# Holding the sums of a fused attention kernel to the plan, moving the first of them to GpSimd, and spreading the half products

## The chip, the cores and the metric

The kernel runs on one core of a Trainium2 chip. The metric is the device time of one execution in microseconds (us), given as the median of several executions. The profile is one execution, recorded instruction by instruction. Engine names are those of the profile: PE is TensorE, PEld its weight loads, DVE is VectorE, ACT is ScalarE, POOL is GpSimd, SP is SyncE. The profile lists a stream of instructions for each engine (8145 on PE and 1788 on DVE in the kernel before) and the semaphore events that ended its waits. What a wait means for DVE is seen in the profile below: while it stood 6.03 us before one instruction, nothing behind that instruction ran on it. The *granted clock* is the share of PE's full clock that the profile records as granted (0.959 in the mean in the kernel before).

## The reference, cut to what matters

```python
# u, v: 8 x 3008 x 256;  z: 8 x 3008 x 64;  w_in: 256 x 2048;  w_out: 2048 x 256
scores = (1/3008) * z @ z.T                 # per batch, symmetric
attn   = maximum(scores, 0) ** 2
x      = u * (attn @ v)                     # 24064 rows of 256
h      = x @ w_in
out    = (h * cos(h)) @ w_out
```

Because `scores` is symmetric, only the tiles with row block R at or after column block c are computed. The others are made by a DMA that transposes a finished tile (the first three columns of the first batch are an exception: all their tiles are computed).

## The kernel before

Each batch has six columns of 512 tokens, numbered from 0 (the last has 448). A column is planned as 8 units of time, and every piece of work is given a place in that plan. The pieces are emitted in the order of the plan; a scheduler then decides the order on each engine. The matmuls are chained, so PE keeps the planned order. The other engines are not chained.

```python
def chain(mm):                       # fixes the order of the PE stream
    if before:
        after(mm.ins, before.pop(), NOSYNC)
    before.append(mm.ins)
```

For columns 2 to 5 (3 to 5 in the first batch) the part of `attn @ v` that uses transposed tiles is made with seven half products instead of eight, for up to four row blocks W ("four-row columns" below are columns 4 and 5). That needs sums of quarters of the tiles. The *first sums* are two per tile, and the first of them writes in place:

```python
def a_sums1(b, c, R):                # 102 tiles, so 204 first sums
    s1 = quarter(b, c, R, 0, 1)
    nc.vector.tensor_tensor(s1, s1, quarter(b, c, R, 1, 1), ALU.add)
    nc.vector.tensor_tensor(
        second(b, c, R), s1, quarter(b, c, R, 0, 0), ALU.subtract)

def a_sums2(b, c, R):                # the second sums, later in the column
    # ...
    nc.vector.tensor_tensor(dst, src, sub, ALU.subtract)
# ... in the plan of a column that begins at unit t:
at(t - 2.5 + 0.5 * i, 2, lambda b=b, c=c, R=R: a_sums1(b, c, R))
at(t + 1.5 + 0.3 * i, 2, lambda b=b, c=c, R=R: a_sums2(b, c, R))
for n, o in ((1, 1.0), (5, 1.0), (2, 1.0), (6, 1.4), (7, 3.0), (3, 3.0), (4, 3.4)):
    at(t + o, 2, lambda b=b, c=c, n=n: product(b, c, n))
    # ... keep(): ACT and DVE take partial products out of PSUM
```

Three more kinds of DVE work matter. The *squares* are `s <- rt * rt`, 128x1024, with both inputs in SBUF. The products *g* are `h * cos(h)`, with one input in PSUM. The *finish x* is `acc * u`, also with one input in PSUM. Six PSUM buffers `w` serve the scores, h and the output; a score visit takes all six. Two buffers `acc` serve the column. GpSimd issues the loads and makes sums of v (`v_sums`).

## Time and profile before

The time before is 1403.17 us (median of 3, 1401.99 to 1404.43). The profiled execution is a further one, of 1409.64 us with a span of 1407.9 us.

| | busy us | share of the span |
|---|---|---|
| PE | 1272.8 | 90% |
| DVE | 955.0 | 68% |
| ACT | 885.3 | 63% |
| POOL | 234.6 | 17% |

PE is the bound. These are the groups of PE instructions of the kernel before that show idle time. The columns are busy time and mean ns of one, then the idle time of PE just before them and what ended it.

```profile
L324 PE MATMUL acc<-s,v 128*128 128x512 f16 (+1 forms) x1392 | 345.2, 386 | 10.4 <-DVE x L347 10.4
L419 PE MATMUL acc<-s,vsum 128*128 128x256 f16 (+1 forms) x816 | 112.5, 279 | 19.5 <-ACT q L439 9.4 <-ACT p L432 8.2 <-DVE s L391 1.0
L236 PE MATMUL w<-zT 64*128 64x512 f16 (+3 forms) x684 | 109.9, 374 | 63.3 <-DVE g L458 46.8 <-DVE rt L267 12.8 <-ACT zT L199 1.6
L419 PE MATMUL acc<-s,v 128*128 128x256 f16 (+1 forms) x612 | 87.2, 286 | 37.5 <-DVE x L347 37.5
```

With 1.2 us before the first matmuls this adds up to 131.9 us of idle PE. About 108 us of it is released by DVE, although DVE is only 68% busy; most of the rest is released by ACT. So DVE is not short of time; it is late at certain moments. PE's timeline of the kernel before at one batch boundary shows two such moments (start, duration, instructions, idle time before):

```profile
660.82 0.60 PE L468 MATMUL w<-w_out,g 128*128 128x256 f16 x4
664.93 1.68 PE L419 MATMUL acc<-s,v 128*128 128x224 f16 x8 [3.51 <-DVE x L347]
...
667.77 0.93 PE L419 MATMUL acc<-s,v 128*128 128x224 f16 x8
...
687.28 0.44 PE L236 MATMUL w<-zT 64*128 64x512 f16 x3
694.44 1.18 PE L236 MATMUL w<-zT 64*128 64x256 f16 x3 [6.72 <-DVE g L458]
```

After the wait eight matmuls of one shape take 1.68 us, where eight of that shape take 0.93 us a little later: the clock was halved (the trace's clock record reads 0.5 from 664.22 to 667.63 us). The DVE timeline of the same stretch tells what DVE was doing:

```profile
655.28 2.48 DVE L458 TENSOR_TENSOR g<-w,c 128x512 f16<-128x512 f32 x4
663.79 0.42 DVE L376 TENSOR_TENSOR s<-s 128x512 f16<-128x512 f16 x1 [6.03 <-DMA s<-s]
664.13 1.41 DVE L347 TENSOR_TENSOR x<-acc,ut 128x192 f16<-128x192 f32 x4
...
685.22 1.28 DVE L458 TENSOR_TENSOR g<-w,c 128x512 f16<-128x512 f32 x2
693.17 0.62 DVE L376 TENSOR_TENSOR s<-s 128x512 f16<-128x512 f16 x1 [6.67 <-DMA s<-s]
693.72 1.27 DVE L458 TENSOR_TENSOR g<-w,c 128x512 f16<-128x512 f32 x2
```

DVE stands at a first sum (L376) whose transposing DMA has not landed, and the finish x or the products g behind it are late by as much. Over the whole span the list of waits has this line (engine and what it waited for: us in total, times, longest):

```profile
DVE s L376 <- DMA s<-s: 199.5, 72, 7.8
```

These sums are not due yet. In the built order the first sum of the second batch stands behind 40 products g on DVE. The scheduler had moved it ahead, since nothing forbade it.

### The profile page before, as it was taken

What the parts mean: (1) busy time and instruction counts of PE and PEld (TensorE: products, weight loads), DVE (VectorE), ACT (ScalarE), POOL (GpSimd) and SP (SyncE); (2) the same over time, 40 slices, a digit from 0 to 9 for tenths busy, and PEclk for the clock granted to TensorE, in tenths of its full rate; (3) what the DMA queues carried; (4) which work ended last, traced back from release to release, by engine and by line L of the source; (5) the groups of instructions that cost most, each with busy time, mean ns of one, the idle gap of its engine ahead of it and who ended that gap; (6) DMA issues with size and microseconds to landing.
All of it is one profiled execution on the core that took longest, in us unless ns stands there. A gap on an engine that the chain in (4) does not pass through costs nothing.

```text
span 1407.9 us, 22304 instructions
## 1 busy us (share of the span) xinstructions
PE 1272.8 (90%) x8145; PEld 752.0 (53%) x8145; DVE 955.0 (68%) x1788; ACT 885.3 (63%) x1702; POOL 234.6 (17%) x329
## 2 busy tenths in 40 slices
PE   6689799997999879998799987999879898899999
PEld 2136555564556545566455654556545565455666
DVE  6677567776667676676666865668656686566865
ACT  4367556665667656675566755666656666566656
POOL 6021310114001040111401013010130101300000
PEclk8799999998999989999999999999999999999999
DMA  9886766686657865766756667576675766756511
GB/s 123 137 113 106 108 104 108 105 121 102 101 104 103 125 104 83 115 109 110 110 90 104 123 92 111 101 96 121 91 111 102 99 116 91 111 102 93 90 39 46
DMA packets 484222, 144.98 MB, mean 103 GB/s; under 512 B 432400, under 2 KB 484112, under 8 KB 484112
## 3 DMA queue, kind: packets, MB, share of 16 engines
q1 hardware_dynamic: 356448, 88.73, 37.4%
q0 software_dynamic: 100400, 29.77, 21.6%
q10 hardware_dynamic: 27264, 25.06, 5.6%
q8 instruction: 64, 1.05, 0.3%
q14 instruction: 46, 0.38, 0.1%
HBM read 60.29 MB, written 24.64 MB: 60 GB/s over the span
## 4 chain that ended last, share of the span: by engine, by line
PE 70%; DMA 16%; DVE 6%; ACT 4%; issue 3%; ACTq 0%; DVEq 0%; SPq 0%
PE w L468 18%; PE w L451 18%; PE acc L324 18%; DMA s<-s 16%; PE acc L419 10%; PE w L236 5%; ACT rt L269 2%; DVE g L458 2%; DVE x L347 1%; DVE s L271 1%; DVE s L391 1%; DVE s L376 1%; PE acc L298 1%; ACT c L455 1%; ACT p L432 0%
## 5 line engine op out<-in xcount | busy, mean ns | idle before, releaser
L455 ACT ACTIVATE c<-w,pihalf 128x512 f16<-128x512 f32 x752 | 502.0, 704 | 300.7 <-PE w L451 209.9
L458 DVE TENSOR_TENSOR g<-w,c 128x512 f16<-128x512 f32 x752 | 491.2, 685 | 89.3 <-ACT c L455 86.1
L468 PE MATMUL w<-w_out,g 128*128 128x256 f16 x3008 | 453.1, 274 | 0.0
L451 PE MATMUL w<-x,w_in 128*128 128x512 f16 x1504 | 452.1, 384 | 0.0
L468 PEld LDWEIGHTS <-g 128*128 128x128 f16 x3008 | 296.5, 99 | 195.9 <-issue 7.0
L324 PE MATMUL acc<-s,v 128*128 128x512 f16 (+1 forms) x1392 | 345.2, 386 | 10.4 <-DVE x L347 10.4
L269 ACT ACTIVATE rt<-w 128x512 f16<-128x512 f32 x489 | 253.7, 615 | 110.8 <-PE w L236 99.4
L271 DVE TENSOR_TENSOR s<-rt 128x1024 f16<-128x1024 f16 x254 | 187.3, 743 | 113.7 <-ACT rt L269 113.5
L324 PEld LDWEIGHTS <-v 128*128 128x128 f16 x1392 | 130.2, 99 | 177.0 <-issue 64.6
L94 POOL DMA_DIRECT2D ust<-in_u_dram x112 | 81.4, 733 | 628.4 <-PE acc L324 617.3
L376 DVE TENSOR_TENSOR s<-s 128x512 f16<-128x512 f16 (+1 forms) x102 | 43.7, 429 | 199.6 <-DMA s<-s 199.5
L451 PEld LDWEIGHTS <-w_in 128*128 128x128 f16 x1504 | 149.0, 99 | 52.9 <-issue 6.7
L236 PE MATMUL w<-zT 64*128 64x512 f16 (+3 forms) x684 | 109.9, 374 | 63.3 <-DVE g L458 46.8
L419 PE MATMUL acc<-s,vsum 128*128 128x256 f16 (+1 forms) x816 | 112.5, 279 | 19.5 <-ACT q L439 9.4
L419 PE MATMUL acc<-s,v 128*128 128x256 f16 (+1 forms) x612 | 87.2, 286 | 37.5 <-DVE x L347 37.5
L419 PEld LDWEIGHTS <-vsum 128*128 128x128 f16 x816 | 79.7, 101 | 51.1 <-issue 42.9
L253 ACT ACTIVATE rt<-w 128x512 f16<-128x512 f32 (+3 forms) x176 | 63.6, 448 | 57.9 <-PE w L236 57.9
L419 PEld LDWEIGHTS <-v 128*128 128x128 f16 x612 | 62.6, 104 | 48.6 <-DVE x L347 37.3
L236 PEld LDWEIGHTS <-zT 64*128 64x128 f16 x684 | 26.0, 95 | 113.3 <-issue 100.6
L475 ACT ACTIVATE ob<-w 128x256 f32<-128x256 f32 x188 | 71.3, 379 | 5.3 <-PE w L468 5.3
L347 DVE TENSOR_TENSOR x<-acc,ut 128x64 f16<-128x64 f32 (+7 forms) x178 | 68.9, 431 | 3.6 <-PE acc L324 3.5
L391 DVE TENSOR_TENSOR s<-s,s 128x1024 f16<-128x1024 f16 (+1 forms) x102 | 62.1, 665 | 7.6 <-PE acc L419 7.6
(38 smaller groups left out, 374.3 us busy)
## 6 DMA issues: line engine op xcount, KB each, us to landing
out_dram<-ob ACTq DMA_DIRECT2D x92, 256.0 KB, 2.2
ust<-in_u_dram POOLq DMA_DIRECT2D x80, 128.0 KB, 5.0
v<-in_v_dram POOLq DMA_DIRECT2D x16, 512.0 KB, 6.5
s<-s SPq DMA_TRANSPOSE x249, 4.3
v<-in_v_dram POOLq DMA_DIRECT2D x8, 448.0 KB, 6.0
zst<-in_z_dram POOLq DMA_DIRECT2D x14, 128.0 KB, 3.8
ust<-in_u_dram POOLq DMA_DIRECT2D x16, 96.0 KB, 4.0
w_in<-in_moe_w_in_dram POOLq DMA_DIRECT2D x4, 256.0 KB, 6.0
```

The source lines that it names most:

```text
L94: hold(nc.gpsimd.dma_start(dst, src))
L236: chain(nc.tensor.matmul(sp[:, s0 * P:], zt[h, R * K + k + 1 - lo, :], zt[h, j0 + s0:j0 + K, :].rearrange("p j w -> p (j w)"), start=True, ...
L269: nc.scalar.activation(rt[:, i, :], banks[k], AF.Relu)
L271: nc.vector.tensor_tensor(t.rearrange("p s k w -> p k s w")[:, 2 * p:2 * p + 2], rv, rv, ALU.mult)
L324: chain(nc.tensor.matmul(acc[nh][:, 0:wn], vs(b, j // G)[:, j % G, nh * P:(nh + 1) * P], a, start=(start and n == 0), stop=(last and n == ...
L347: nc.vector.tensor_tensor(x[:, nh, :], acc[nh][:, o:o + n], ut[:, nh, o:o + n], ALU.mult)
L391: nc.vector.tensor_tensor(dst, src, sub, ALU.subtract)
L419: chain(nc.tensor.matmul(acc[bank][:, cols], lhs[:, k, :], rhs[:, k, :], start=(n in (1, 5) and i == k == 0), stop=(i == len(W) - 1 and k ...
L451: chain(nc.tensor.matmul(hp, w_in16[:, k, ft * P:(ft + 1) * P], x[:, k, :], start=(k == 0), stop=(k == NDH - 1)))
L455: nc.scalar.activation(c16, hp, AF.Sin, bias=pihalf, scale=inv_s2)
L458: nc.vector.tensor_tensor(gs[(m, ft // FG)][:, ft % FG, :], hp, c16, ALU.mult)
L468: chain(nc.tensor.matmul(ys[m][:, 0:D], gs[(m, f4)][:, ft % FG, ts * P:(ts + 1) * P], w_out16[:, ft, :], start=(ft == 0), stop=(ft == NFT ...
```

## The change

The change does three things. It holds `a_sums1`, `a_sums2` and the sums of v to the last matmul emitted before them. This is an order for the scheduler, not a semaphore. It moves the two first sums of each tile from VectorE to GpSimd. And it spreads the seven products over the column, with the full matmuls of each bank between them; the buffers of the tiles are kept longer for that.

```diff
     def a_sums1(b, c, R):
         s1 = quarter(b, c, R, 0, 1)
-        nc.vector.tensor_tensor(s1, s1, quarter(b, c, R, 1, 1), ALU.add)
-        nc.vector.tensor_tensor(
+        after(nc.gpsimd.tensor_tensor(s1, s1, quarter(b, c, R, 1, 1), ALU.add).ins,
+              before[-1], NOSYNC)
+        nc.gpsimd.tensor_tensor(
             second(b, c, R), s1, quarter(b, c, R, 0, 0), ALU.subtract)
 ...   (a_sums2 and the first instruction of v_sums get the same after(...))
+    PLAN = {2: [(1.0, 'P1 P5 P2'), (2.35, 'P6'), (3.0, 'B4 P7'), (3.4, 'P3 B2'), (4.35, 'P4'), ...],
+            3: [...], 4: [(1.0, 'P1 P5'), (1.4, 'P2'), (2.35, 'P6'), (3.0, 'B3'), (3.4, 'P7'), ...]}
 ...   (P1 to P7 are the products; A4 is four full matmuls on the first bank, B4 on the second)
-                for n, o in ((1, 1.0), (5, 1.0), (2, 1.0), (6, 1.4), (7, 3.0), (3, 3.0), (4, 3.4)):
-                    at(t + o, 2, lambda b=b, c=c, n=n: product(b, c, n))
+                for o, what in PLAN[len(W)]:
+                    for piece in what.split():
 ...
+                at(t + 7.45, 2, lambda b=b, c=c: finish(b, c))
```

More of the change, by code (lines that the diff above doesn't have):

```diff
@@ L49 @@
     NW = 4
+    PLAN = {2: [(1.0, 'P1 P5 P2'), (2.35, 'P6'), (3.0, 'B4 P7'), (3.4, 'P3 B2'), (4.35, 'P4'), (5.0, 'A5'), (5.4, 'B3'), (7.0, 'A6 B3'), (7.4, 'A4 B3')], 3: [(1.0, 'P1 P5'), (1.4, 'P2'), (2.35, 'P6'), (3.0, 'B4 P7'), (3.4, 'P3'), (4.35, 'P4'), (5.0, 'A4'), (5.4, 'B3'), (7.0, 'A4'), (7.4, 'A3 B4')], 4: [(1.0, 'P1 P5'), (1.4, 'P2'), (2.35, 'P6'), (3.0, 'B3'), (3.4, 'P7'), (4.35, 'P3'), (5.0, 'P4'), (5.4, 'B2'), (7.0, 'A4'), (7.4, 'A3 B2')]}
+    SUM1, SUM2, WADD = (-2.5, 0.5), (1.5, 0.3), 3.5
+    HALF = 4.0
     inv_s = 1.0 / float(S)
@@ L315, in open_acc, with av_bank @@
         accs[(b, c)] = [ps_acc.tile([P, CW], FP32, name="acc") for nh in range(NDH)]
+    def av_bank(b, c, nh, blocks, start, last):
+        acc = accs[(b, c)][nh]
+        for n, j in enumerate(blocks):
+            wn, a = moving(b, c, j)
+            chain(nc.tensor.matmul(
+                acc[:, 0:wn],
+                vs(b, j // G)[:, j % G, nh * P:(nh + 1) * P], a,
+                start=(start and n == 0), stop=(last and n == len(blocks) - 1),
+                skip_group_check=True))
     def av_chunk(b, c, blocks, start, last):
@@ L319, in av_chunk @@
             open_acc(b, c)
-        acc = accs[(b, c)]
         for nh in range(NDH):
-            for n, j in enumerate(blocks):
-                wn, a = moving(b, c, j)
-                chain(nc.tensor.matmul(
-                    acc[nh][:, 0:wn],
-                    vs(b, j // G)[:, j % G, nh * P:(nh + 1) * P], a,
-                    start=(start and n == 0), stop=(last and n == len(blocks) - 1),
-                    skip_group_check=True))
+            av_bank(b, c, nh, blocks, start, last)
         if last:
@@ L357, in v_sums @@
         o = vsum[R]
-        nc.gpsimd.tensor_tensor(o[:, 0], t[:, k1, d2], t[:, k1, d1], ALU.subtract)
+        after(nc.gpsimd.tensor_tensor(o[:, 0], t[:, k1, d2], t[:, k1, d1],
+                                      ALU.subtract).ins, before[-1], NOSYNC)
         nc.gpsimd.tensor_tensor(o[:, 2], t[:, k2, d2], t[:, k1, d2], ALU.subtract)
@@ L390, in a_sums2 @@
         sub = x.unsqueeze(1).broadcast_to([P, 2, 2, h])
-        nc.vector.tensor_tensor(dst, src, sub, ALU.subtract)
+        after(nc.vector.tensor_tensor(dst, src, sub, ALU.subtract).ins,
+              before[-1], NOSYNC)
     parts_of = {}
@@ L544 @@
             ready = 1.5 + when[(b, c, NC - 1)]
-            first, last = (0.6, 6.93) if d else (4.0 if W else 1.0, 7.3)
+            first, last = (0.6, 6.93) if d else (HALF if W else 1.0, 7.3)
             room = [i for i, sc in enumerate(scores)
@@ L560 @@
                 for i, R in enumerate(W):
-                    at(t - 2.5 + 0.5 * i, 2, lambda b=b, c=c, R=R: a_sums1(b, c, R))
-                    use(("x", b, c), t - 2.5, t + 3.0)
-                    use(("t", b, R, c), t, t + 3.6)
-                    at(t + 1.5 + 0.3 * i, 2, lambda b=b, c=c, R=R: a_sums2(b, c, R))
-                for n, o in ((1, 1.0), (5, 1.0), (2, 1.0), (6, 1.4), (7, 3.0), (3, 3.0), (4, 3.4)):
-                    at(t + o, 2, lambda b=b, c=c, n=n: product(b, c, n))
-                    if n in (1, 5, 6, 7):
-                        at(t + o + 0.02, 2, lambda b=b, c=c, n=n: keep(b, c, n))
@@ L569 @@
-                at(t + 3.45, 2, lambda b=b, c=c: keep(b, c, 0))
-                n = len(blocks)
-                sizes = {15: [2, 4, 3, 4, 2], 11: [1, 3, 2, 3, 2], 7: [0, 2, 2, 2, 1]}[n]
-                places = list(zip((t + o for o in (3.42, 5.0, 5.4, 7.0, 7.4)), sizes))
+                    at(t + SUM1[0] + SUM1[1] * i, 2, lambda b=b, c=c, R=R: a_sums1(b, c, R))
+                    use(("x", b, c), t + SUM1[0], t + 4.0)
+                    use(("t", b, R, c), t, t + 6.5)
+                    at(t + SUM2[0] + SUM2[1] * i, 2.5, lambda b=b, c=c, R=R: a_sums2(b, c, R))
@@ new lines @@
+                at(t + WADD, 2.6, lambda b=b, c=c: keep(b, c, 0))
+                done = [0, 0]
+                for o, what in PLAN[len(W)]:
+                    for piece in what.split():
+                        if piece[0] == "P":
+                            n = int(piece[1])
+                            at(t + o, 2, lambda b=b, c=c, n=n: product(b, c, n))
+                            if n in (1, 5, 6, 7):
+                                at(t + o + 0.02, 2.1, lambda b=b, c=c, n=n: keep(b, c, n))
+                            continue
+                        nh, size = "AB".index(piece[0]), int(piece[1:])
+                        part = blocks[done[nh]:done[nh] + size]
+                        done[nh] += size
+                        end = done[nh] >= len(blocks)
+                        at(t + o, 2, lambda b=b, c=c, nh=nh, part=part, end=end:
+                           av_bank(b, c, nh, part, False, end))
+                        for j in part:
+                            R = j // K
+                            use(("a", b, c, R) if R >= c else ("t", b, R, c), t + o, t + o + 0.3)
@@ L573 @@
+                assert done == [len(blocks)] * 2, (done, len(blocks))
+                at(t + 7.45, 2, lambda b=b, c=c: finish(b, c))
+                places = []
             else:
```

## The prediction

> **What bounds the kernel now.** TensorE. The page: PE busy 1272.8 of 1407.9 us (90%), DVE 955.0, ACT 885.3, POOL 234.6. PE's groups show 132 us idle: 63.3 before the score matmuls (46.8 released by DVE's g products), 47.9 before accumulator matmuls released by DVE's finish (x), 17.6 released by the ACT copies p and q. PE's timeline shows where: at each of 7 batch boundaries one wait of 3.5 to 5.3 us (DVE x) and one of 5.3 to 7.0 us (DVE g), 72 us together. In the DVE timeline both have one cause: DVE stands 5 to 7 us before a first sum (128x512) whose transposing DMA has not landed (199.5 us, 72 waits in the list of waits; not all cost PE anything). The scheduler hoisted those sums up to a dozen units of the plan ahead of their place in the program, and the in-order DVE then holds back g and x, and with them PSUM. After each such wait matmuls run at half clock for 3 to 4 us (at 664.93, 8 matmuls in 1.68 us instead of 0.93). [...] Estimate: 24 us in all.
>
> **What the change does.**
> 1. Holds the sums to points of the PE stream (in the built order no first sum is early now). The boundary waits go: 72 + 24 us. The x waits of the third column (8.7 us, with half clock 12) and part of the start (8) go too: about 115 us.
> 2. Spreads the half products, so that p and q are copied before products 6 and 4: 15 of 17.6 us.
> 3. Moves 204 first sums (386 to 446 ns, 82 us) off DVE. POOL's 128x256 sums take 0.66 us, so I estimate 1.1 to 1.3 us each, 240 us: POOL about 475 us. PE's work is unchanged (8145 matmuls).
>
> **What it costs.** In four-row columns POOL does up to 7 sums and 4 load issues between a load held 2 units before the column and product 5: 11 us against about 11 us of PE time; I count 10 us of waits. [...] squares (128x1024, 0.69 us) took 1.16 and 0.85 us beside POOL sums, and once, at the start, 10.4 us through a back-to-back run of them. I estimate 60 us of added DVE time, half of it felt by PE, because a score visit needs all six PSUM buffers: 25 to 30 us.
>
> **Sum.** 1403 - 115 - 15 + 10 + 25 = 1308; PE's median start-to-start times sum to about 1265, the floor. Prediction 1304 us, range 1272 to 1348. Faster by over 2%: 0.90; within 2%: 0.07; slower: 0.03.
>
> **What would show it.** Right: no DVE wait on the s transposes; both boundary waits gone from PE's timeline; granted clock there from 0.88 to about 1; PE over 95% busy; DVE still 900 to 940 us in spite of 82 us less work; POOL's first sums 1.1 to 1.3 us; squares' mean over 743 ns. Wrong: DVE waits on POOL, or PE on POOL at product 5 or 6.
>
> **What would make it wrong.** [...] several us of PE wait plus half clock, some 30 times, would return most of the gain. Or DVE is freed so well that PE gets near 1275.

Three passages are cut from the prediction; words are cut from the expectations of e1, e3 and e6. The sum: 1403 - 115 - 15 + 10 + 25 = 1308. Its 25 rests on the times of the squares alone: the 60 us of added DVE time were my estimate from squares of 0.85 and 1.16 us beside a GpSimd sum, where 0.69 is usual, and the half of it felt by PE was an estimate too. The words before "several us of PE wait" named squares held up in every four-row column as the one of 10.4 us was. The "3 to 4 us" at half clock are rough: in the clock record half clock goes on for 2.7 to 5.6 us after the fourteen boundary waits.

## More of the kernel before

The squares of the kernel before, for comparison with the changed one:

```profile
L271 DVE TENSOR_TENSOR s<-rt 128x1024 f16<-128x1024 f16 x254 | 187.3, 743 | 113.7 <-ACT rt L269 113.5
```

## The result, and the profile after

The changed kernel takes 1314.63 us (median of 3, 1314.48 to 1315.11). The ratio to the kernel before is 0.937, with a 95% interval of 0.9348 to 0.9391. Ratios here are the mean time of one kernel's fast runs over that of the other's of the same rounds, so not quite the ratio of the medians quoted. The profiled execution was one of these three, with a span of 1312.7 us. Its busy times, from the page:

```profile
PE 1239.5 (94%) x8145; PEld 743.2 (57%) x8145; DVE 991.1 (76%) x1584; ACT 877.5 (67%) x1702; POOL 475.0 (36%) x533
```

The span fell by 95.2 us from one profile to the other (the medians by 88.5). PE idle fell from 131.9 to 70.1 us, and PE busy by 33.3 us with the same 8145 matmuls. The second part goes with the clock: the mean granted clock rose from 0.959 to 0.991, so the share withheld fell from 57.7 us (4.1% of the span) to 11.8 us. PE's groups with idle time, of the changed kernel:

```profile
L428 PE MATMUL acc<-s,vsum 128*128 128x256 f16 (+1 forms) x816 | 109.9, 274 | 14.6 <-DVE acc L445 11.5 <-POOL s L383 2.9
L239 PE MATMUL w<-zT 64*128 64x512 f16 (+3 forms) x684 | 96.0, 359 | 4.6 <-DVE g L467 2.0 <-ACT zT L202 1.6 <-DVE zT L204 0.5
L428 PE MATMUL acc<-s,v 128*128 128x256 f16 (+1 forms) x612 | 84.5, 279 | 46.5 <-DVE x L353 23.5 <-ACT p L441 11.4 <-DVE acc L451 11.4
```

The wait for g is down from 46.8 to 2.0 us and there is no DVE wait for the transposing DMA any more. But two readings do not fit a simple gain. DVE lost 204 instructions, which took 82 us before, and is busy for 36 us *more* than before. And PE still waits 23.5 us for the finish x. The group of the squares says where the DVE time went: mean 1102 ns, where the kernel before had 743.

```profile
L274 DVE TENSOR_TENSOR s<-rt 128x1024 f16<-128x1024 f16 x254 | 276.7, 1102 | 133.8 <-ACT rt L272 132.0
```

The timeline of the changed kernel just before a four-row column shows one of them:

```profile
573.49 2.27 POOL L383 TENSOR_TENSOR s<-s 128x512 f16<-128x512 f16 x2
...
575.19 4.44 DVE L274 TENSOR_TENSOR s<-rt 128x1024 f16<-128x1024 f16 x1 [1.32 <-ACT rt L272]
575.71 2.26 POOL L385 TENSOR_TENSOR s<-s 128x512 f16<-128x512 f16 x2
...
577.93 1.14 POOL L383 TENSOR_TENSOR s<-s 128x512 f16<-128x512 f16 x1
...
579.15 1.49 POOL L385 TENSOR_TENSOR s<-s 128x512 f16<-128x512 f16 x1
579.55 1.98 DVE L257 TENSOR_TENSOR s<-rt 128x512 f16<-128x512 f16 x4
...
581.45 1.41 DVE L353 TENSOR_TENSOR x<-acc,ut 128x192 f16<-128x192 f32 x4
582.25 1.25 PE L428 MATMUL acc<-s,v 128*128 128x256 f16 x8 [2.64 <-DVE x L353]
```

A square of 0.69 us took 4.44 us while GpSimd made its sums. The diagonal squares, the finish x and product 1 of the column all came late behind it. A wait of this kind returns at the same place in every batch (2.56 to 2.65 us, in the last one 5.13).

Sorting the trace's records by whether a GpSimd sum ran at the same time gives a control within the run (mean ns, changed kernel; the last column is the count that overlaps times the difference):

```
                         alone            beside a POOL sum   added us
square 128x1024          177 x  689         77 x 2051          104.9
diagonal square 128x512   30 x  424         14 x  999            8.1
g (one input in PSUM)    524 x  685        228 x  682            0
x (one input in PSUM), all widths: alone and beside within 4 ns  0
all DVE tensor operations                                      117.7
```

In this trace only operations with both inputs in SBUF take longer beside a sum (and not all: seven second sums of 128x896 took 616 ns beside one and 618 alone). In the kernel before the same sum of added time is 15.1 us.

The records show two more things about these squares. The eight of 4.4 us pass four sums between which no gap is recorded, and end 0.56 us after the fourth, where 78 to 79 ns pass before the fifth sum starts. And GpSimd's DMA issues seem to take part. The 33 squares beside DMA issues alone took 690 ns, but seven squares of 2.81 to 2.82 us met one sum of 1.16 us with a DMA issue of 0.78 us right behind it, and ended 0.33 us after that issue.

### The profile page after: what moved, and what is told of

It reads as the page before. It is cut to its first block, busy times and chain, and to the rows that moved or that the text cites. A ratio compares the mean times of both kernels' runs of the same rounds, so it can differ in the third digit from the quotient of the medians.

```text
span 1312.7 us, 22453 instructions
## 1 busy us (share of the span) xinstructions
PE 1239.5 (94%) x8145; PEld 743.2 (57%) x8145; DVE 991.1 (76%) x1584; ACT 877.5 (67%) x1702; POOL 475.0 (36%) x533
## 4 chain that ended last, share of the span: by engine, by line
PE 65%; DVE 16%; ACT 8%; issue 7%; DMA 4%; POOL 1%; DVEq 0%; ACTq 0%; POOLq 0%
PE w L477 17%; PE w L460 17%; PE acc L324 17%; PE acc L428 9%; ACT rt L272 5%; DVE s L274 5%; DVE g L467 5%; PE w L239 4%; DMA v<-in_v_dram 3%; DVE x L353 2%; DVE s L257 1%; DVE s L399 1%; ACT c L464 1%; DMA ut<-ust 1%; ACT rt L256 1%
## 5 line engine op out<-in xcount | busy, mean ns | idle before, releaser
L477 PE MATMUL w<-w_out,g 128*128 128x256 f16 x3008 | 448.6, 273 | 0.0
L460 PE MATMUL w<-x,w_in 128*128 128x512 f16 x1504 | 447.6, 380 | 0.0
L274 DVE TENSOR_TENSOR s<-rt 128x1024 f16<-128x1024 f16 x254 | 276.7, 1102 | 133.8 <-ACT rt L272 132.0
L324 PE MATMUL acc<-s,v 128*128 128x512 f16 (+1 forms) x1392 | 337.8, 378 | 1.6 <-DVE x L353 1.6
L324 PEld LDWEIGHTS <-v 128*128 128x128 f16 x1392 | 128.9, 98 | 151.1 <-issue 38.0
L428 PE MATMUL acc<-s,v 128*128 128x256 f16 (+1 forms) x612 | 84.5, 279 | 46.5 <-DVE x L353 23.5
L385 POOL TENSOR_TENSOR s<-s 128x512 f16<-128x512 f16 (+1 forms) x102 | 120.9, 1191 | 3.6
L383 POOL TENSOR_TENSOR s<-s 128x512 f16<-128x512 f16 (+1 forms) x102 | 117.6, 1160 | 0.7
L239 PE MATMUL w<-zT 64*128 64x512 f16 (+3 forms) x684 | 96.0, 359 | 4.6 <-DVE g L467 2.0
L428 PEld LDWEIGHTS <-v 128*128 128x128 f16 x612 | 59.4, 101 | 65.2 <-issue 34.5
L257 DVE TENSOR_TENSOR s<-rt 128x512 f16<-128x512 f16 (+3 forms) x176 | 62.3, 409 | 27.3 <-ACT rt L256 27.3
L97 POOL DMA_DIRECT2D v<-in_v_dram x40 | 32.1, 807 | 120.5 <-PE acc L428 76.2
```

Source lines behind the costliest of these rows:

```text
L97: hold(nc.gpsimd.dma_start(dst, src))
L239: chain(nc.tensor.matmul(sp[:, s0 * P:], zt[h, R * K + k + 1 - lo, :], zt[h, j0 + s0:j0 + K, :].rearrange("p j w -> p (j w)"), start=True, ...
L274: nc.vector.tensor_tensor(t.rearrange("p s k w -> p k s w")[:, 2 * p:2 * p + 2], rv, rv, ALU.mult)
L324: chain(nc.tensor.matmul(acc[:, 0:wn], vs(b, j // G)[:, j % G, nh * P:(nh + 1) * P], a, start=(start and n == 0), stop=(last and n == len( ...
L383: after(nc.gpsimd.tensor_tensor(s1, s1, quarter(b, c, R, 1, 1), ALU.add).ins, before[-1], NOSYNC)
L385: nc.gpsimd.tensor_tensor(second(b, c, R), s1, quarter(b, c, R, 0, 0), ALU.subtract)
```

## The experiments

The theory before the first run, A: what pays is the hold, because it takes the waits for the DMA out of the middle of the DVE queue. The move to GpSimd costs time, because squares take longer beside sums on GpSimd (in the kernel before 0.85 and 1.16 us instead of 0.69, and once 10.4). The rivals were B, that the relief of DVE by 82 us pays, and C, that the spread pays. All runs were correct against the reference and, except for one execution named below, fast, that is within 1.5% of the fastest execution of the same kernel. The runs were made on three chips, e1 to e4, e5 to e8 and e9 to e10, on which the kernel before took 1402.6, 1407.6 and 1405.5 us (medians); so a difference of medians from two of these groups is sure to about 5 us only.

### 1 to 4: the parts alone

e1, the changed kernel with its first sums back on VectorE, still held:

```diff
-        after(nc.gpsimd.tensor_tensor(s1, s1, quarter(b, c, R, 1, 1), ALU.add).ins,
+        after(nc.vector.tensor_tensor(s1, s1, quarter(b, c, R, 1, 1), ALU.add).ins,
               before[-1], NOSYNC)
-        nc.gpsimd.tensor_tensor(
+        nc.vector.tensor_tensor(
```

> The changed kernel, but its first sums go back to VectorE, still held. Theory A (the hold pays[...]): no wait of DVE on POOL sums, squares back to a mean near 690 ns, the 2.6 us wait of PE before product 1 in four-row columns gone, 1285 to 1308 us, not slower than the changed kernel (1314.6). Theory B (the relief of VectorE by 82 us pays): VectorE waits for transposing DMAs again or is late with g, 1330 us or more.

Measured: 1255.83 us, ratio 0.8946 (0.891 to 0.8982). This is 59 us faster than the changed kernel, and beyond the range that theory A gave. B falls: DVE needs no relief. One of the four executions, the profiled one, took 2554.46 us and is left out; see e5 and the last section.

e2, the kernel before with only the hold:

```diff
-        nc.vector.tensor_tensor(s1, s1, quarter(b, c, R, 1, 1), ALU.add)
+        after(nc.vector.tensor_tensor(s1, s1, quarter(b, c, R, 1, 1), ALU.add).ins,
+              before[-1], NOSYNC)
 ...   (a_sums2 and v_sums likewise)
```

> The kernel before with the hold alone: sums on VectorE, old plan of the products. Theory A: both waits at the batch boundaries gone, 1290 to 1320 us, that is 85 to 110 us of the 88.5 us gained. Theory B: 1370 us or more.

Measured: 1284.65 us, ratio 0.9157 (0.9118 to 0.9197), 5 us below the range that theory A gave. The hold, with no computing instruction added or moved to another engine, gives 118 us, more than the whole change. It orders three kinds of sums, which no run here separates; the DMA waits that it removes stood before the first sums. PE idle is 44.5 us, most of it here:

```profile
L422 PE MATMUL acc<-s,vsum 128*128 128x256 f16 (+1 forms) x816 | 115.7, 276 | 36.9 <-DVE s L393 23.0 <-ACT p L435 8.4 <-ACT q L442 5.4
```

e3, the kernel before with only the move:

```diff
-        nc.vector.tensor_tensor(s1, s1, quarter(b, c, R, 1, 1), ALU.add)
-        nc.vector.tensor_tensor(
+        nc.gpsimd.tensor_tensor(s1, s1, quarter(b, c, R, 1, 1), ALU.add)
+        nc.gpsimd.tensor_tensor(
```

> The kernel before with the first sums on GpSimd, not held, old plan. Theory A: hoisted sums now make GpSimd stand, not VectorE, so the boundary waits go here too, but loads behind the sums come late[...]: 1315 to 1360 us. Theory B: 1320 us or less.

Measured: 1323.44 us (1315.45 to 1332.02), ratio 0.9431 (0.9377 to 0.9486). The waits for the DMA have not gone; they have changed engine. The list of waits of this run:

```profile
POOL s L376 <- DMA s<-s: 347.2, 82, 10.3
```

GpSimd may stand there without holding g or x back, so most of the boundary waits go (the longest PE wait of the whole span is 2.8 us, where the boundary waits were up to 7.0). The added DVE time is 94.6 us. The median lies in the range of theory A and only 3 us above that of B, so this run alone hardly separates them; e1 does.

e4, the kernel before with only the spread (the changed kernel without the hold, sums on VectorE):

```diff
-        after(nc.gpsimd.tensor_tensor(s1, s1, quarter(b, c, R, 1, 1), ALU.add).ins,
-              before[-1], NOSYNC)
-        nc.gpsimd.tensor_tensor(
+        nc.vector.tensor_tensor(s1, s1, quarter(b, c, R, 1, 1), ALU.add)
+        nc.vector.tensor_tensor(
 ...   (and no after(...) in a_sums2 and v_sums)
```

> The kernel before with the spread products alone: sums on VectorE, not held. Theory A: only the ACT waits of 17.6 us can go, boundary waits stay: 1385 to 1402 us. Rival C (the spread is what pays): 1340 us or less.

Measured: 1391.95 us, ratio 0.9917 (0.9883 to 0.9952), 11 us by the medians. The boundary waits stand as before (DVE still waits 175.9 us for the transposing DMA). C falls.

### 5 to 8: is it the reading?

e5 repeats e1's kernel unchanged, for a profile of a normal execution.

> The same kernel as in the first experiment, for a profile of a normal execution (there the profiled one took 2554 us, about twice the other three). Expected 1250 to 1262 us again; a second execution of 2500 us would make the anomaly the kernel's own. In the profile: PE idle under 35 us in all, no PE wait over 1.5 us after the first 60 us, squares' mean 700 ns or less.

Measured: 1257.49 us (1256.63 to 1259.8), ratio 0.8938 (0.8907 to 0.8969), no slow execution. The page's busy times, the squares and one of the two groups of first sums, now on DVE, and PE's two groups of half products:

```profile
PE 1226.3 (97%) x8145; PEld 741.5 (59%) x8145; DVE 950.9 (76%) x1788; ACT 883.4 (70%) x1702; POOL 237.2 (19%) x329
L274 DVE TENSOR_TENSOR s<-rt 128x1024 f16<-128x1024 f16 x254 | 178.5, 709 | 128.5 <-ACT rt L272 126.7
L383 DVE TENSOR_TENSOR s<-s 128x512 f16<-128x512 f16 (+1 forms) x102 | 40.8, 406 | 0.0
```

```profile
L428 PE MATMUL acc<-s,vsum 128*128 128x256 f16 (+1 forms) x816 | 105.9, 268 | 12.9 <-DVE acc L445 12.9
L428 PE MATMUL acc<-s,v 128*128 128x256 f16 (+1 forms) x612 | 80.2, 270 | 5.5 <-DVE acc L451 4.6 <-ACT p L441 0.9
```

With 204 more instructions than in the changed kernel, DVE is busy for 40 us less. PE idle is 28.4 us in all, and the mean granted clock 0.997. The squares' mean is 709 ns, not the 700 or less expected, because the sums of v still run on GpSimd (the 19 squares beside them took 0.95 us in the mean). One wait of 1.80 us in the first batch remains after 60 us; from the second batch on none is over 1.0.

e6 and e7 keep this kernel and give GpSimd work that nobody needs, at the same points. In e6 it reads and writes, in e7 it only writes.

```diff
+    scr = [kpool.tile([P, CW], FP16, name=f"scr{i}") for i in range(2)]      # e7: [P, 1280]
 ...   (at the end of a_sums1, whose sums are on VectorE)
+        for i in range(2):
+            after(nc.gpsimd.tensor_tensor(
+                scr[i], w_in16[:, 0, 0:CW], w_in16[:, 1, 0:CW], ALU.add).ins,
+                before[-1], NOSYNC)
+        # e7 instead: after(nc.gpsimd.memset(scr[i], 0.0).ins, before[-1], NOSYNC)
```

Theory P, in the expectations: what GpSimd's additions do to the VectorE operations beside them is the whole cost of the move.

> Sums held on VectorE as in the run above, and GpSimd makes at the same points 204 additions of 128x512 whose results nobody uses. Theory P[...]: 1300 us or more, although no engine waits for a result of GpSimd, and squares that overlap with these additions take over 1.5 us in the mean. Theory L (PE and VectorE wait for late sums): within 10 us of the run above, 1250 to 1265 us.

> As the run with unused additions, but GpSimd only fills 128x1280 elements each time (it writes and reads nothing; an estimated 1.1 us each from the 0.2 us of 128x128). Theory P, in the form that only reads collide: within 10 us of the run without them, 1250 to 1265 us, squares at 690 ns. If any access of GpSimd collides, or if its loads come late behind the work: 1290 us or more.

Measured: with the unused additions 1427.15 us, ratio 1.0141 (1.0106 to 1.0176), that is 170 us lost. With the fills 1256.23 us, ratio 0.8925 (0.8893 to 0.8957), nothing lost. The work on GpSimd was of the same length in both, first e6:

```profile
L389 POOL TENSOR_TENSOR scr<-w_in 128x512 f16<-128x512 f16 x204 | 241.3, 1214 | 0.4
```

and in e7:

```profile
L389 POOL MEMSET scr<- 128x1280 f16 x204 | 230.2, 1195 | 0.0
```

In e7 the 50 squares beside fills alone took 690 ns; in e6 the 21 beside the unused additions took 2.30 us in the mean. Nobody waits for a result of these additions, and the fills occupy GpSimd about as long (230 us against 241). So the cost came with the additions, which read SBUF, and not with the fills, which only write, and theory L, that PE waits for late sums, is not needed. By what mechanism an addition holds up VectorE is not shown by these runs. In the changed kernel itself PE waited only 2.9 us for a sum on GpSimd. The loss in e6 is larger than the 59 us of the move. Its trace shows two differences that fit: VectorE has its own first sums to be slowed as well (their two groups took 1229 and 1023 ns in the mean, where e5 has 406 and 407), and the additions do not depend on each other and run without gaps (0.4 us of idle before all 204). One of the two groups of first sums in e6:

```profile
L384 DVE TENSOR_TENSOR s<-s 128x512 f16<-128x512 f16 (+1 forms) x102 | 124.8, 1229 | 0.0
```

This timeline of e6 shows a first sum of 0.42 us that waits through four of them, first POOL's part:

```profile
619.48 6.93 POOL L389 TENSOR_TENSOR scr<-w_in 128x512 f16<-128x512 f16 x6
```

then DVE's:

```profile
620.88 1.27 DVE L472 TENSOR_TENSOR g<-w,c 128x512 f16<-128x512 f32 x2
622.08 4.61 DVE L384 TENSOR_TENSOR s<-s 128x512 f16<-128x512 f16 x1
626.73 0.42 DVE L386 TENSOR_TENSOR s<-s 128x512 f16<-128x512 f16 x1
```

The two products g before it, with one input in PSUM, took 1.27 us together under the same POOL run; two at 612.93 us with no GpSimd instruction beside them took 1.28 us. The sum ends 0.3 us after the run.

e8, the changed kernel with the old plan of the products (hold and move, no spread). Its edit is e2's with `gpsimd` in place of `vector` in the first sums.

> The changed kernel with the old plan of the products. From the runs so far the move to GpSimd cost 59 us on the new plan. If it costs the same on the old plan, 1284.7 + 59 = 1343 us; if the spread plan is there to hide the late sums of GpSimd, more than 1360 us; under 1325 us would say that the spread gains nothing once GpSimd makes the sums.

Measured: 1337.43 us, ratio 0.95 (0.9463 to 0.9538). The move costs 53 us on the old plan (1337.4 against 1284.7) and 59 us on the new one, so its cost hardly depends on the plan.

### 9 and 10: runs of sums, and the hold on GpSimd

In the changed kernel the sums lie in runs without a gap, because the load at 2 units before the column holds GpSimd up and the sums behind it then follow at once: GpSimd had stood 18.81 us before the load at 569.68 us, and from there to 579.07 us its loads and first sums follow each other with at most 0.03 us between them. e9 keeps them apart: each waits by semaphore for its own point of the PE stream.

```diff
-    SUM1, SUM2, WADD = (-2.5, 0.5), (1.5, 0.3), 3.5
+    SUM1, SUM2, WADD = (-4.5, 1.0), (1.5, 0.3), 3.5
 ...   (a_sums1 is split into its two steps, emitted half a unit apart; each gets)
+        after(i.ins, before[-1], SYNC)
```

> The changed kernel with its GpSimd sums kept apart: each of them waits by semaphore for its own point of the PE stream, half a unit (about 1.6 us) after the one before it, the first 4.5 units before the column. Theory R (a square that meets a gapless run of GpSimd sums waits for the whole run): longest square under 2.5 us instead of 4.45, added VectorE time 40 to 75 us instead of 118, the 2.6 us wait before product 1 gone, 1270 to 1300 us. Theory T (each us of GpSimd reading costs the same, runs or not): 1305 us or more.

Measured: 1278.97 us, ratio 0.9097 (0.9069 to 0.9124), 36 us better than the changed kernel with the same work on the same engines. The squares of the changed kernel (durations in ns: least, median, longest):

```profile
L274 DVE TENSOR_TENSOR s<-rt x254: 674/693/4454, 8.4 to 1226.9; 128x1024 f16<-128x1024 f16 x127
```

and of e9:

```profile
L274 DVE TENSOR_TENSOR s<-rt x254: 674/693/2301, 8.4 to 1198.7; 128x1024 f16<-128x1024 f16 x127
```

The longest wait is halved, the added DVE time is 79 us instead of 118 (a little over the range expected), and PE waits only 1.9 us for the finish x in all. Theory T falls, and the result fits theory R: the runs matter. But e9 also moves the sums up to 2 units earlier and so lets them meet other DVE work; the two effects are not separated. And it is still some 22 us behind the sums on VectorE.

e10, the changed kernel without the hold (sums on GpSimd, products spread; e3's edit on the new plan):

> The changed kernel without the hold: sums on GpSimd, products spread. Theory A (the hold pays because it takes the wait for the transposing DMA out of the VectorE queue; once the sums are on GpSimd that wait is out of it anyway): 1300 to 1325 us, so the hold adds little on GpSimd. If the hold's gain of 118 us is independent of the engine: 1370 us or more.

Measured: 1330.77 us, ratio 0.9473 (0.9432 to 0.9515), 6 us above the range given. On GpSimd the hold gains 16 us with the new plan. With the old one e8, held, is 14 us slower than e3, but the intervals of their ratios overlap, so this is not clear of noise. On VectorE the hold gains 118 us.

All medians side by side:

| sums on | old plan, not held | old plan, held | spread, not held | spread, held |
|---|---|---|---|---|
| VectorE | 1403 (before) | 1284.7 (e2) | 1392.0 (e4) | 1255.8, 1257.5 (e1, e5) |
| GpSimd | 1323.4 (e3) | 1337.4 (e8) | 1330.8 (e10) | 1314.6 (the change) |

The parts do not simply add: the move costs 53 to 59 us where the sums are held, and gains some 60 to 80 us where they are not, because it takes the wait for the DMA out of the DVE queue as the hold does. The best kernel is e1: the change without its move to GpSimd.

## Why the prediction was right or wrong

The time lay in the range (1272 to 1348) and 11 us from the point. The direction and the mechanism were right. The terms of the sum were right to different degrees.

- *The hold.* "About 115 us" for the hold: right for the sums on VectorE, where alone it gives 118 us (e2). With the sums already on GpSimd it is worth 16 us (e10), because the move has by then removed most of the same waits. The waits for the transposing DMA, both boundary waits and the half clock after them went as foretold.
- *How far the sums had been hoisted.* "Up to a dozen units": too small; the built order says 22.
- *The spread.* "15 of 17.6 us": right in size only for the spread alone (11 us, e4). With the hold it gives 27 to 29 us on VectorE (e2 against e5 and e1) and 23 us on GpSimd (e8 against the change). In e2 23.0 of 36.9 us of idle before the products with summed v were waits for the second sums of the column; the spread takes those away too, and the prediction had not counted them.
- *The cost of GpSimd.* "10 + 25": this is the step that was mis-sized. The move costs 53 to 59 us. The direct wait of PE on POOL was put too high (2.9 us against 10). The added DVE time was put at 60 us and is 118, of which 15 were there before the change, because I counted about one sum per collision. In the changed trace 51 of the 59 DVE operations that took over 1.5 us overlapped two or more sums, and eight of them five. The sign for it was in the profile before: the square of 10.4 us under a run of 16 sums of v, which I took for a tail risk.
- *The relief of DVE.* The sum of the prediction gave it nothing, and rightly: 82 us of DVE work moved away, and the kernel got slower by 59.
- *The floor.* "About 1265" is no floor: e1 took 1255.8 us with the same matmuls.
- *The signs.* Right: no DVE wait for the DMA, POOL 475.0 us, its first sums 1.16 and 1.19 us, squares over 743 ns (1102), both boundary waits gone, and full clock at the boundaries (half clock is recorded only at 67.5, 258.7, 583.0, 1071.1 and 1234.9 us, at waits inside the batches, and at the end). Wrong: DVE is 991 us busy, not 900 to 940; PE is 94% busy, just under the 95% named. Of the signs named for a failure, PE did wait for POOL, but only twice.

That the sum came out near is in part luck: a spread that gained 14 us more than predicted stood against a move that cost about 24 us more (59 against 35).

## What to carry to other kernels

DVE, 68% busy, cost PE 72 us of waits at the seven batch boundaries here, because at each an instruction that waited for a DMA stood too early in its queue; the hold gained 118 us (e2). Where an engine that is not full holds up another, look at what ended its waits, compare the place of that instruction in the built order with the place where its input is ready, and pin it before moving any work away. Before giving elementwise work to GpSimd, list what VectorE does at the same time: here it had operations with two SBUF inputs, the work was not free (53 to 59 us where the sums are held), and a gapless run held up a square for 4.45 us, where the spaced sums of e9 gave 2.30 us at most. And a change of several parts should be measured part by part, since here one part took back 59 of the 147 us that the other two gained.

## What the traces showed of the hardware

- GpSimd additions and fills differed: 204 additions of 1.21 us cost 170 us, 204 fills of 1.20 us nothing (e6, e7), and products g, with an input in PSUM, keep their 0.68 us beside a sum.
- Starting first did not always save a square: in the changed kernel 22 squares that started 0.17 to 0.59 us before the earliest GpSimd sum they met took 1.16 to 2.82 us all the same, and only 5 squares that started before such a sum took 0.81 us or less. (Recorded spans of GpSimd are rough: a sum recorded to end at 571.66 us is followed by an issue that starts at 571.59.) A VectorE instruction can be passed by several GpSimd instructions in a row: 4.45 us under a run of sums in the changed kernel, 10.4 us under 16 sums of v at the start of the kernel before, up to 13.5 us in e6. At other times it gets in after the current one (1.16 us). In the squares of 4.4 and 10.4 us it got in where 78 to 79 ns without a GpSimd instruction are recorded, but squares of 1.16 us of the kernel before got in with no recorded gap; what decides between the two is left open here.
- A DMA issue of GpSimd did not slow a square alone (690 ns), but seems to prolong a wait that a sum began (2.81 us, seven squares of the changed kernel).
- The estimate of 1.1 to 1.3 us for a first sum on GpSimd, from the 0.66 us of a 128x256 sum, held: in fp16 the two groups of 128x512 sums took 1.19 and 1.23 us in the mean.
- Around and after the boundary waits the clock record of the kernel before reads 0.5 (8 matmuls in 1.68 us after a wait of 3.51 us, 0.93 later). The profiled execution of e1 took 2552.5 us with PE 100% busy and no clock record at all (the profile's page reads 1.0), and its 512-column matmuls started 443 ns apart, where e5, the same program, has 216. Matmuls of this width at half clock start 427 ns apart in the kernel before, so most of it looks like half clock for the whole execution. It came once in eight executions of this program, and its cause is open.
